# Attention sums of two units at once, with half blocks as 64-row products and TensorE in order of emission

## The chip, the cores and the metric

The kernel runs on one core of a Trainium2 chip. The metric is the device time of one execution in microseconds. A profiled execution gives the trace; its times are microseconds from the span's start.

The core has TensorE (PE; its loading of stationary operands is PEld), VectorE (DVE), ScalarE (ACT), GpSimd (POOL) and SyncE (SP), which issues the DMAs here. A matrix product on TensorE takes a stationary and a moving operand from SBUF and adds into a bank of PSUM; VectorE and ScalarE read the banks.

## The reference

Windowed causal attention, then a two-layer MLP with a gelu, over 8 batches of 576 tokens, 8 heads of 64:

```
scores = q @ k^T / 8 + alibi bias;  only the 128 keys up to and with the query count
attn   = softmax(scores)            (+ 1e-9 in the denominator)
x      = (attn @ v), heads side by side -> [4608, 512]
out    = gelu(x @ w_in) @ w_out     (w_in 512 x 2048, w_out 2048 x 512)
```

All is float32 outside. Inside, most operands are split into a high and a low float16 part (hi, lo), and a product is three float16 products: hi*hi, hi*lo, lo*hi.

## The kernel before

**Two tilings.** The MLP works on 9 tiles of 512 tokens (`t`), attention on 8 batches of 576 (`b`). A batch's 9 blocks of 64 queries (`j`) fall on two tiles: part 0 on tile `b`, part 1 on tile `b + 1` (`blocks_of`). A query block sees three key blocks of 64, its own and the two before. Heads are worked in pairs; a unit is one head pair of one batch, so a batch has four units, 0 to 3.

**A unit's way.** `scores` (L496) writes 9 groups of 128 x 192 scores into five PSUM banks; its matmuls use 64 rows and 64 columns of the array, with four of them going round (two heads, two halves of the output). `biased` (L548) scales the scores on VectorE and adds the bias; that frees the banks. `softmax` (L633) takes maxima on VectorE, exponentials on ScalarE, the high weights on GpSimd; `low_weights` (L652) makes the low parts on VectorE, and a DMA transposes the weights from `e_main` into `et` (L658), keys on partitions: 128 keys to a slot. `weigh` (L675) sums the values: the stationary operand is 128 keys x 64 features of one head (`vbuf`), the moving one the turned weights of one block of 64 queries, or of two neighbouring blocks (128 columns) where both are in the part, and a unit's results lie in two banks, one per part. Of the 128 keys of a slot a block often sees the upper or the lower 64 alone; the other half holds zeros. `leave` (L708) copies a bank to `x` as hi on ScalarE (L720) and lo on VectorE (L721, recorded at the helper's line L218).

**Order.** The first two tiles and batches follow an order written out by hand. From tile 2 on a loop (L1250) goes through 32 steps a tile, `t` = 2 to 6 with batch `b = t + 1`. Steps 0 to 15 are `mlp_in` (12 products of 512 columns into `h`, L747) and `gelu`; steps 16 to 31 are 12 products each of `mlp_out` (`o`, L793). In between, units' scores come after the products of steps 2, 11, 16 and 21 (`SCORES_AT`; tile 2: the first at 4, batch 7: the last at 22) and their sums and leaving after steps 12, 20, 30 and 30 (`WEIGH_AT`; tile 2: the first at 13). This is an order of emission: a scheduler puts each engine's instructions in order by a simulated time line, emission order being the priority. An engine works through its own list strictly in that order. Tile 7 has no attention, and tile 8 is worked by other functions.

**Banks.** PSUM's eight banks are two pools of four. `att` holds the first, second and fourth of a unit's score banks, and the sums; `mm` holds the other two score banks (`FIFTH`), `h` and `o`.

## Time and profile before

| | us |
|---|---|
| three runs: median (lowest to highest) | 880.13 (879.61 to 880.25) |
| the profiled execution, its span | 879.11, 877.3 |
| TensorE busy in the span | 861.7 (98%) |
| VectorE busy | 709.3 (81%) |
| ScalarE busy | 546.5 (62%) |
| GpSimd busy | 196.0 (22%) |
| products h (L747), busy | 337.7 |
| products o (L793), busy | 258.3 (192.4 + 65.9) |
| attention sums av (L700), busy | 42.7 |

Busy time of a group is the union of its instructions' times, so matmuls that run beside each other are not counted twice. A line of the timeline is a run of like instructions of one engine: its start, how long until the last one's end, the line, the operation, the names, the first one's shape, and the count. A matmul's end lies some 0.2 to 0.4 us behind its start, so what a run costs is read from its start to the next run's start.

### The profile page before, as it was taken

To read this page: it belongs to the slowest core of one execution; us is meant where nothing else is said; L and a number is where in the kernel's file an instruction comes from. 1 tells how busy PE (TensorE), PEld (TensorE's weight loads), DVE (VectorE), ACT (ScalarE), POOL (GpSimd) and SP (SyncE) were. 2 spreads that over 40 slices of the span, in tenths; PEclk is the share of its full clock that TensorE was granted. 3 is DMA by queue.
4 is the path that set the end of the run, shared out by engine and by line. 5 is a ranking of instruction groups with operands and counts; after the bars stand their busy time and mean duration, and the time that the engine had idled before them with its cause. 6 is when DMAs were issued, how large, how long until landed. Compare 5 with 4: busy or idle time off the path is not lost.

```text
span 877.3 us, 18582 instructions
## 1 busy us (share of the span) xinstructions
PE 861.7 (98%) x7428; PEld 476.9 (54%) x7428; DVE 709.3 (81%) x1388; ACT 546.5 (62%) x1147; POOL 196.0 (22%) x412
## 2 busy tenths in 40 slices
PE   6999999999999999999999999999999999999998
PEld 4644445544554545454545545445545554588887
DVE  6999999999768984887578775878477889998871
ACT  8999879896755573465464455466355338644760
POOL 0011000222015440452126421543054310000000
PEclk9999999999999999999999999999999999999999
DMA  9766645452572346233622473225122330001001
GB/s 311 268 208 230 228 117 133 134 168 62 132 233 38 73 97 203 57 69 77 187 72 56 93 171 117 55 55 118 39 56 56 78 67 13 0 13 37 1 1 49
DMA packets 174598, 91.63 MB, mean 104 GB/s; under 512 B 133680, under 2 KB 156336, under 8 KB 174384
## 3 DMA queue, kind: packets, MB, share of 16 engines
q1 hardware_dynamic: 174512, 90.45, 38.3%
q8 instruction: 58, 0.95, 0.4%
q14 instruction: 28, 0.23, 0.1%
HBM read 46.53 MB, written 9.44 MB: 64 GB/s over the span
## 4 chain that ended last, share of the span: by engine, by line
PE 70%; DVE 12%; ACT 2%; DMA 2%; issue 2%; POOL 1%; SPq 0%; ACTq 0%; POOLq 0%; DVEq 0%
PE h L747 27%; PE o L793 24%; PE av L700 4%; PE u_out L1082 4%; PE sc L529 3%; PE u L995 2%; DVE e_main L218 2%; DMA et<-e_main 2%; PE v L995 2%; DVE nmax L638 1%; DVE s L555 1%; PE z_out L1082 1%; PE x_out L1082 1%; PE y_out L1082 1%; PE v_out L1082 1%
## 5 line engine op out<-in xcount | busy, mean ns | idle before, releaser
L747 PE MATMUL h<-x,wi 128*128 128x512 f16 x1536 | 337.7, 379 | 1.1 <-ACT g L769 0.6
L747 PEld LDWEIGHTS <-wi 128*128 128x128 f16 x1536 | 148.5, 98 | 181.2 <-issue 4.0
L793 PE MATMUL o<-wo,g 128*128 128x512 f16 x864 | 192.4, 379 | 0.0
L793 PEld LDWEIGHTS <-g 128*128 128x128 f16 x1152 | 110.9, 98 | 132.8 <-issue 0.3
L641 ACT ACTIVATE s<-s,nmax 128x192 f32<-128x192 f32 x252 | 110.8, 441 | 46.3 <-DVE nmax L638 46.1
L218 DVE SCALAR_TENSOR_TENSOR e_main<-s,z,e_main 128x192 f16<-128x192 f32 x252 | 116.3, 505 | 15.2 <-POOL e_main L650 10.4
L771 POOL TENSOR_SCALAR g<-g,sg 128x512 f16<-128x512 f32 x96 | 76.8, 806 | 228.0 <-ACT g L769 200.8
L769 ACT ACTIVATE g<-h,gs 128x512 f32<-128x512 f32 x96 | 64.0, 686 | 95.9 <-PE h L747 59.1
L218 DVE SCALAR_TENSOR_TENSOR g<-g,sg,g 128x512 f16<-128x512 f32 x96 | 80.1, 851 | 34.0 <-POOL g L771 33.8
L650 POOL TENSOR_SCALAR e_main<-s,z 128x192 f16<-128x192 f32 x180 | 89.1, 514 | 66.9 <-ACT s L641 37.9
L555 DVE SCALAR_TENSOR_TENSOR s<-sc,cs,bias_h 128x384 f32<-128x384 f32 x112 | 64.2, 608 | 10.1 <-PE sc L529 9.9
L793 PE MATMUL o<-wo_first,g 128*128 128x512 f16 x288 | 65.9, 379 | 0.0
L720 ACT ACTIVATE x<-av,cx 128x448 f16<-128x448 f32 (+6 forms) x52 | 24.3, 481 | 62.0 <-PE av L700 59.5
L790 PE MATMUL o<-zo,g 128*128 128x512 f32 x128 | 57.0, 597 | 0.0
L638 DVE TENSOR_REDUCE nmax<-s 128x5 f32<-128x960 f32 (+1 forms) x56 | 56.6, 1043 | 0.4 <-POOL s L561 0.3
L529 PE MATMUL sc<-kbuf,qbuf 64*64 64x192 f16 (+3 forms) x1656 | 48.3, 250 | 7.6 <-ACT qbuf L431 4.4
L561 POOL MEMSET s<- 64x128 f32 (+1 forms) x112 | 19.2, 172 | 142.3 <-DVE s L555 131.2
L218 DVE SCALAR_TENSOR_TENSOR x<-av,cx,x 128x448 f16<-128x448 f32 (+6 forms) x52 | 24.7, 493 | 28.5 <-ACT x L720 28.4
L641 ACT ACTIVATION_READ_ACCUMULATOR s<-s,nmax 128x1 f32 x252 | 47.1, 187 | 0.0
L700 PEld LDWEIGHTS <-vbuf 128*64 128x64 f16 x1680 | 40.4, 111 | 9.4 <-issue 8.8
L700 PE MATMUL av<-et,vbuf 128*64 128x128 f16 (+1 forms) x1680 | 42.7, 210 | 0.4 <-DMA et<-e_main 0.3
L1082 PEld LDWEIGHTS <-g 128*128 128x128 f16 x384 | 37.6, 98 | 4.6
(269 smaller groups left out, 1126.3 us busy)
## 6 DMA issues: line engine op xcount, KB each, us to landing
v<-vp SPq DMA_DIRECT2D x32, 320.0 KB, 5.2
out<-ob SPq DMA_DIRECT2D x34, 256.0 KB, 2.2
raw<-w_in SPq DMA_DIRECT2D x8, 1024.0 KB, 11.0
raw<-w_out SPq DMA_DIRECT2D x8, 1024.0 KB, 6.7
q<-qp SPq DMA_DIRECT2D x7, 1152.0 KB, 6.0
k<-kp SPq DMA_DIRECT2D x7, 1152.0 KB, 7.5
qbuf<-qp SPq DMA_DIRECT2D x4, 288.0 KB, 5.4
kbuf<-kp SPq DMA_DIRECT2D x4, 288.0 KB, 5.7
```

The costliest lines, as they stand in the source:

```text
L218: return nc.vector.scalar_tensor_tensor(out=dst, in0=src, scalar=scale, in1=high, op0=ALU.mult, op1=ALU.subtract)
L529: done = nc.tensor.matmul(ps[bank][o, n, gap:W], a, m[:, gap:W], start=(i == 0 and (n == 0 or b > 0)), stop=(i == len(terms) - 1 and b > 0 ...
L555: yield nc.vector.scalar_tensor_tensor(out=s[:, bank[0] : bank[0] + k, :], in0=ps[bank][:, 0:k, 0:W], scalar=cs, in1=bias.broadcast_to([P, ...
L638: yield nc.vector.tensor_reduce(out=nmax[:, r], in_=s[:, r], axis=AX.X, op=ALU.max, negate=True)
L641: yield nc.scalar.activation(s[:, i, :], s[:, i, :], AF.Exp, bias=nmax[:, i : i + 1], accum_out=z[:, i : i + 1])
L650: yield nc.gpsimd.tensor_scalar(e[:, i, 0, c], s[:, i], z[:, i : i + 1], 1.0, op0=ALU.mult, op1=ALU.mult)
L700: done = nc.tensor.matmul(av[r, (j - blocks[0]) * QB : (j - blocks[0] + len(js)) * QB], v32s[b][:, hp, kb, r] if b < EXACT else vbuf[:, vi ...
L747: done = nc.tensor.matmul(ph, wi[n][:, a, cc, k * P : (k + 1) * P], x[:, cc, b, :], start=(i == 0), stop=(i == 3 * NCC - 1),)
L769: yield nc.scalar.activation(g32, ph, AF.Gelu, scale=gsc[t, n])
L771: yield nc.gpsimd.tensor_scalar(g[:, r, 0], g32, gsg[t, n], 1.0, op0=ALU.mult, op1=ALU.mult)
L793: done = nc.tensor.matmul(o, g[:, r, a, c], wo[n][:, b, k, :], start=(fc == first and i == 0), stop=(fc == last and i == 2),)
L1082: nc.tensor.matmul(ps[name][:, tb], f(d, a)[:, k, tb * P : (tb + 1) * P], w(d, b, k), start=first, stop=True, skip_group_check=True,)
```

## The change

A new function sums the values for two units at a time, from batch 3 on (in batch 7 for units 0 and 1 alone; units 2 and 3 keep `weigh` and `leave`). Every product has 64 columns, one block of queries. Where a block sees only 64 of the 128 keys of a slot, the product takes 64 rows: even blocks the lower 64, odd blocks from 3 on the upper 64. Results lie in up to four banks of `att`: by part, and within it by even and odd blocks, each with both units side by side. The list of products: for the two units and the three terms, the lower halves of both heads, after each pair of them (as long as there are any) a pair of upper halves; then the full ones. The generator stops once, between halves and full ones.

```
+    def weigh_two(one, two):
...
+        for part, odd in banks:
+            one.av[part, odd] = bank_of([P, TT], "att" if b else "mm", f"av{one.u}_{b + part}_{odd}")
...
+        low = [(st, u, t, j // 2, 1, j) for st, u, t in each for j in range(0, NB, 2)]
+        high = [(st, u, t, (j - 3) // 2, 0, j) for st, u, t in each for j in range(3, NB, 2)]
+        for n, (st, u, t, *at) in enumerate(low):
+            for h in range(2):
+                job(slice(0, D), st, u, h, *t, *at)
+            if n < len(high):
+                st, u, t, *at = high[n]
+                for h in range(2):
+                    job(slice(D, P), st, u, h, *t, *at)
+        halves = len(todo)
+        for st, u, t in each:
+            for j in range(1, NB):
+                for h in range(2):
+                    job(slice(0, P), st, u, h, *t, (j - 1) // 2, j % 2, j)
+        started = set()
+        for n, (key, o, a, m) in enumerate(todo):
+            if n == halves:
+                yield done
+            left[key] -= 1
+            done = nc.tensor.matmul(o, a, m, start=key not in started, stop=left[key] == 0, skip_group_check=True)
+            started.add(key)
+        yield done
```

Leaving takes one copy per bank for both units on ScalarE, and one low part per bank and unit on VectorE:

```
+    def leave_two(one, two):
...
+                yield nc.scalar.activation(dst(0, (0, 1)), av, AF.Copy, scale=c)
+                for u in range(2):
+                    yield low_part(dst(1, (u,)), av[:, u], c, dst(0, (u,)))
```

In the loop, units 0 and 1 are summed after step 18 (tile 2: 19) and units 2 and 3 after step 30; in batch 5 the half blocks come one step before that. The loop runs under an order of emission for TensorE:

```
-    SCORES_AT, WEIGH_AT = (2, 11, 16, 21), (12, 20, 30, 30)
+    SCORES_AT, WEIGH_AT, APART = (2, 11, 16, 21), (18, 30), (5,)
...
+        with tc.manual_schedule(engines={mybir.EngineType.PE}):
+            for step in range(2 * NFC):
...
-            for hp in range(NPAIR):
-                if weigh_at[hp] == step:
-                    for part in range(2):
-                        run(weigh(unit(b, hp), [part]))
-                        run(leave(unit(b, hp), [part]))
...
+                for n, at in enumerate(weigh_at):
+                    two = [unit(b, 2 * n + k) for k in range(2)]
+                    if n and b == B - 1:
...
+                        continue
+                    if step == at - (b in APART):
+                        weighing = weigh_two(*two)
+                        next(weighing)
+                    if step == at:
+                        next(weighing)
+                        run(leave_two(*two))
```

## Rows read from the trace of the kernel before

**Rows 1.** The page: busy time, share, instructions; the granted clock in 40 slices.
```profile
PE 861.7 (98%) x7428; PEld 476.9 (54%) x7428; DVE 709.3 (81%) x1388; ACT 546.5 (62%) x1147; POOL 196.0 (22%) x412
...
PEclk9999999999999999999999999999999999999999
```
**Rows 2.** The page: the chain that ended last, by engine.
```profile
PE 70%; DVE 12%; ACT 2%; DMA 2%; issue 2%; POOL 1%; SPq 0%; ACTq 0%; POOLq 0%; DVEq 0%
```
**Rows 3.** Two stretches of tile 4, 460 to 519 us: busy us by engine, summed.
```profile
sum 59.00, PE 59.00 PEld 29.24 DVE 50.31 ACT 32.86 POOL 28.35; mean PE 29.50 PEld 14.62 DVE 25.16 ACT 16.43 POOL 14.18
```
**Rows 4.** Timeline of TensorE in batch 4: start us, us, engine, line, operation.
```profile
392.94 1.28 PE L529 MATMUL sc<-kbuf,qbuf 64*64 64x192 f16 x54
394.14 7.94 PE L793 MATMUL o<-wo,g 128*128 128x512 f16 x36
401.93 2.75 PE L793 MATMUL o<-wo_first,g 128*128 128x512 f16 x12
404.61 1.55 PE L700 MATMUL av<-et,vbuf 128*64 128x128 f16 x54
406.09 2.76 PE L793 MATMUL o<-wo,g 128*128 128x512 f16 x12
...
433.41 2.91 PE L700 MATMUL av<-et,vbuf 128*64 128x128 f16 x108
436.25 0.39 PE L793 MATMUL o<-wo,g 128*128 128x512 f16 x1
```
**Rows 5.** Timeline of TensorE in batch 5.
```profile
475.25 1.60 PE L700 MATMUL av<-et,vbuf 128*64 128x128 f16 x66
...
498.91 1.60 PE L700 MATMUL av<-et,vbuf 128*64 128x128 f16 x66
500.44 2.76 PE L793 MATMUL o<-wo,g 128*128 128x512 f16 x12
...
527.75 3.00 PE L700 MATMUL av<-et,vbuf 128*64 128x128 f16 x132
530.69 0.39 PE L793 MATMUL o<-wo,g 128*128 128x512 f16 x1
```
**Rows 6.** Groups by shape: low parts of leaving, count, busy us, mean ns.
```profile
L218 DVE SCALAR_TENSOR_TENSOR x<-av,cx,x 128x320 f16<-128x320 f32 x8 | 4.4, 545 | 7.9 <-ACT x L720 7.9
L218 DVE SCALAR_TENSOR_TENSOR x<-av,cx,x 128x256 f16<-128x256 f32 x8 | 3.8, 477 | 6.5 <-ACT x L720 6.4
...
L218 DVE SCALAR_TENSOR_TENSOR x<-av,cx,x 128x192 f16<-128x192 f32 x8 | 3.2, 411 | 6.2 <-ACT x L720 6.2
...
L218 DVE SCALAR_TENSOR_TENSOR x<-av,cx,x 128x128 f16<-128x128 f32 x4 | 1.4, 342 | 6.0 <-ACT x L720 6.0
```
**Rows 7.** Transposing DMAs (L658), 460 to 490 us: first and last issue, landing.
```profile
L658 SPq DMA_TRANSPOSE et<-e_main x4: 1589/2094/2562, 463.5 to 487.7; - x4
...
DMA to landing us min/median/max: 3.7/3.9/4.5
```
**Rows 8.** Timeline of VectorE in batches 5 (two rows), 3 and 4.
```profile
488.70 0.60 DVE L218 SCALAR_TENSOR_TENSOR x<-av,cx,x 128x384 f16<-128x384 f32 x1
...
491.65 1.13 DVE L555 SCALAR_TENSOR_TENSOR s<-sc,cs,bias_h 128x384 f32<-128x384 f32 x2
...
314.41 0.93 DVE L218 SCALAR_TENSOR_TENSOR x<-av,cx,x 128x320 f16<-128x320 f32 x2
...
409.51 1.14 DVE L555 SCALAR_TENSOR_TENSOR s<-sc,cs,bias_h 128x384 f32<-128x384 f32 x2 [1.74 <-PE sc L529]
```
**Rows 9.** Timeline of TensorE in batch 3, with a wait.
```profile
283.65 5.34 PE L747 MATMUL h<-x,wi 128*128 128x512 f16 x24 [0.57 <-ACT g L769]
...
314.22 1.49 PE L529 MATMUL sc<-kbuf,qbuf 64*64 64x192 f16 x54
315.65 0.61 PE L793 MATMUL o<-wo,g 128*128 128x512 f16 x2
```

## The prediction

> **What bounds the kernel now.** The first view is the page's busy shares with the clock line: TensorE is busy 98% of the span, VectorE 81%, and the granted clock is full from end to end [rows 1]. The second is the chain that ended last: 70% of it is TensorE [rows 2]. The third is the stretch view, for the change touches one stage, tiles 2 to 6, and the shares of the whole span need not hold there: in 59 us of tile 4, TensorE works all 59.0 us, VectorE 50.3, ScalarE 32.9 [rows 3]. So a microsecond less on TensorE shortens the run, unless TensorE then has to wait for somebody; VectorE, the next, has 15% to spare. The fourth is TensorE's order of time: products stand without a gap, and the attention sums (av, L700) and scores (sc, L529) are bursts between them [rows 4, 5].

> The profiled execution took 879.11 us (span 877.3, 1.8 around it), 1.02 below the median of 880.13. Sums are made against 879.11 and carried over to the median by adding 1.02.

> **What a burst costs now.** From its first start to the next product's start a burst of sums takes 1.48 us with 54 matmuls (batches 4 and 6) and 1.53 with 66 (3 and 5); the two units at the end of a batch take 2.84 with 108 and 2.94 with 132 [rows 4, 5]. Ahead of it 0.09 are lost: 12 o products before a burst take 2.68 us, where 36 without one after them take 7.79, or 2.60 for 12 [rows 4]. The second half of a double burst adds 2.84 - 1.48 = 1.36 (even batches) or 2.94 - 1.53 = 1.41 (odd). By the code a unit of an even batch is 21 head pairs of 128 columns and 6 of 64, one of an odd batch 15 and 18; the two equations give 56 ns a wide pair and 32 ns a narrow one. What is left is 0.21 us per burst for getting into it and out (1.48 - 1.36 + 0.09).

> What changes costs now, with the 0.09: an even batch 2 x 1.57 + 2.93 = 6.07, an odd one 2 x 1.62 + 3.03 = 6.27, the first two units of batch 7 (60 matmuls each, between the two kinds) 1.60 each. Together 2 x 6.07 + 2 x 6.27 + 3.2 = 27.9 us.

> **What it costs then.** Two units become 192 matmuls of 64 columns: by the order of the list 18 quartets (both heads on the lower 64 rows, both on the upper), 12 pairs on the lower rows alone, 48 pairs on all 128. Sixty pairs at 32 ns are 1.92 us. A quartet of 64 columns occurs nowhere before. The score matmuls are quartets of mostly 192: 392.94 to 394.14 with the 0.09 ahead, less 0.21, is 1.08 us for 13.5 quartets, 80 ns each, and 192 columns at the rate of the o products (7.79 us for 36 of 512) are 81 ns [rows 4]. So there four tiles ran at once. The bounds for 64 columns are 27 ns (that column rate) and 64 (two pairs one after the other); I take 33, because the quartets of 192 paid nothing for being four: 0.59 us. The step from 64-row to 128-row products inside a burst is new: 0 to 0.21, I take half, 0.1. Two units: 1.92 + 0.59 + 0.21 + 0.1 = 2.82. In batch 5 the halves are a burst of their own, one step earlier: 2.51 + 2 x 0.21 = 2.93. Seven double bursts at 2.82 and two at 2.93 are 25.6 us: 2.3 saved, part by one burst less per batch, part by the upper half blocks running beside the lower.

> [...]

> **The other edits.** TensorE in order of emission costs nothing by itself: the trace already has scores, o x36, o x12, av, o x12 [rows 4], which is what the loop emits from step 16 on; what it takes away is that a late burst can be passed. Leaving two units: ScalarE keeps 4 copies, with as many columns. VectorE goes from 4 low parts to 8, of 342 ns at 128 columns, 411 at 192, 477 at 256, 545 at 320 [rows 6]. For batch 3 that is 2 x (411 + 3 x 342) = 2.9 us where 2 x (545 + 477) = 2.0 were: +0.8 for two units, 1.7 a batch, into the 15% that VectorE has free. It costs nothing while no bank and no x is waited for. At a batch's end the cover is 12 o products (2.6 us) and the six h products (1.3) that come before x's third feature block is read; a chain of a copy and four low parts, the copy taken like a low part, needs some 2.2. If that cover goes, the first h waits.

> **The new waits.** The sums now take four score banks at once, at step 18 (19 in batch 3, 17 in batch 5), and need the turned weights of unit 1. Behind a late one all products are queued, as TensorE keeps its order.
> Batch 5: the burst at 498.91 ended step 20; three steps of 2.6 and 0.09 before it, at 491.0, step 17 ended. Without the first unit's burst at 475.25 [rows 5] that is 1.62 earlier, 489.4. Unit 1's last transposing DMA went out at 487.7 and took 3.7 at the least, to 491.4 [rows 7]; VectorE read the last score bank of unit 2 that the sums need until 492.2, the first of its two reads at 491.65 [rows 8]. Both chains lose a low part of unit 0 ahead of them (0.60 [rows 8]), and gelu inputs come up to 1.62 earlier, so the wait is between 0 and 1.9; I take 0.6, nearer to the end that has both reliefs. Batches 4, 6 and 7 have a step more, 2.6 us: no wait.
> Batch 3: unit 3's scores waited already, 1.43 us to the next product [rows 9] against 1.20 [rows 4], for unit 1's leaving, which VectorE did at 314.4, behind the e_main low parts [rows 8]. The sums come a step earlier now but put twice the low parts into that queue: 0 to 1.5. I take the 0.2 as gone and nothing new.
> Total: -2.3 - 0.2 + 0.6 = -1.9: 877.2 for the profiled execution, 878.2 for the median.

> **Rivals.**
> 1. *The banks come late.* For it: 1.7 us a batch are added on VectorE, and forced order lets nothing pass. Against: in batch 4 VectorE stood idle for 1.74 us just before unit 3's scores [rows 8], room for most of the new low parts. With 1.9 in batch 5, 1.3 in batch 3 and 0.7 in the others together, 3.9 - 2.3 = +1.6 at worst; half of these waits gives -0.3, 879.8.
> 2. *Quartets of 64 columns run as two pairs* (the slower side). Place: 18 quartets in each of nine double bursts; price 31 ns each, 5.0 us: 883.2. It turns the sign from 33 + 1.9/0.162 = 45 ns a quartet on. Against it stand the score quartets; for it, that each tile changes its weights three times as often as there.
> 3. *No wait at all, and cheap changes of mode.* Quartets at 27 (-1.0), inner step 0 (-0.7), no wait in batch 5 (-0.6), and batch 3's 0.57 for ScalarE [rows 9] gone too: 875.3 at the end, with half of it 876.8.
> [...]

> **Numbers.** Chances: forecast 0.48 (877.0 to 879.2), late banks 0.25, quartets as pairs 0.12, no wait 0.13, floor 0.02. A difference under 0.2% (1.76 us, so 878.4 to 881.9) counts as no change, about what a measurement of this kernel can tell. Faster: three quarters of the forecast and all of rival 3, 0.49. Slower: rivals 2 and 4 and a quarter of the late banks, 0.20. Same: the rest, 0.31. The range goes from near rival 3's far end to rival 2: 875.6 to 883.2.

> **What would show it.** Double bursts of 192 matmuls, some 2.7 us from the first start to the next product's, two per batch (four short ones in batch 5); 3.3 means quartets as pairs. TensorE's waits: av in batch 5 under 1 us, for VectorE's reading or the transposing DMA; sc in batch 3 none. VectorE's busy time up by some 7 us. The forecast is wrong if TensorE's waits in tiles 2 to 6 pass 2 us, or if a tile's first h waits for x.

## Result and the profile after

The changed kernel takes 885.44 us (median of 6 runs, 884.83 to 886.59) against 880.19 of the kernel before on the same chip: ratio 1.0061, 95% interval 1.0048 to 1.0074. It is slower by 5.3 us, where 2 us less were forecast, and it lies above the forecast's range (875.6 to 883.2). The profiled execution took 884.83 us with a span of 883.0, that is 5.7 over the span of before.

The page of the kernel after, the lines that answer to [rows 1] and [rows 2]: busy time by engine, the granted clock, the chain that ended last.
```profile
PE 860.3 (97%) x8076; PEld 474.9 (54%) x8076; DVE 714.5 (81%) x1422; ACT 543.4 (62%) x1146; POOL 197.4 (22%) x412
...
PEclk9999999999999999999999999999999999999999
...
PE 53%; DVE 23%; ACT 6%; issue 4%; DMA 2%; POOL 1%; SPq 0%; POOLq 0%; ACTq 0%; DVEq 0%
```
TensorE is busy 1.4 us less, as a cheaper sum should make it, and the clock is as full as before. But the chain now runs through VectorE for 23% of the span where it was 12%. TensorE waits, and the stretch view says how much. The columns are the stretch, its length, and the busy time (and count) of TensorE, its weight loads, VectorE, ScalarE and GpSimd; first the kernel before, then the one after.
```profile
300.00:700.00 400.00, 399.99 (x3560) 199.30 (x3559) 300.37 (x626) 209.23 (x469) 139.07 (x288) 1.00 0.38 92
```
```profile
300.00:700.00 400.00, 393.01 (x4205) 195.02 (x4206) 299.18 (x649) 204.46 (x467) 139.14 (x285) 1.00 0.37 91
```
In these 400 us TensorE of before stands still for 0.01 us, that of after for 7.0. TensorE's waits in the kernel after (line, what ended the wait, sum, times, longest) name the places:
```profile
PE h L825 <- DVE x L218: 5.5, 4, 1.6
...
PE av L757 <- issue: 0.9, 1, 0.9
...
PE sc L529 <- DVE x L218: 0.4, 1, 0.4
```
None of the three is in the list of before (the scores' wait of before, 1.43 us from start to start against 1.20, does not show in it). The first is the forecast's own sign of failure: "if a tile's first h waits for x". It comes once at the head of each of batches 4 to 7. The timeline of TensorE at the end of batch 3 in the kernel after (start, us, engine, line, operation):
```profile
339.05 2.78 PE L757 MATMUL av<-et,vbuf 64*64 64x64 f16 x192
341.76 2.76 PE L871 MATMUL o<-wo,g 128*128 128x512 f16 x12
344.36 1.89 PE L825 MATMUL h<-x,wi 128*128 128x512 f16 x8
347.86 2.32 PE L825 MATMUL h<-x,wi 128*128 128x512 f16 x10 [1.61 <-DVE x L218]
```
The sums are done at 341.7. Then come 12 o products and 8 h products as cover (the forecast had counted 6; two more read only the high part of the third feature block of x), and the ninth h product stands for 1.6 us, because the low part of that block is not written. ScalarE, then VectorE, in the same 8 us show why:
```profile
341.62 2.43 ACT L421 ACTIVATE vbuf<-v,scv 128x2560 f16<-128x2560 f32 x1 [12.90 <-PE av L757]
343.95 1.66 ACT L782 ACTIVATE x<-av,cx 128x256 f16<-128x256 f32 x4
...
344.08 2.88 DVE L218 SCALAR_TENSOR_TENSOR vbuf<-v,scv,vbuf 128x2560 f16<-128x2560 f32 x1 [10.18 <-ACT vbuf L421]
346.88 2.29 DVE L218 SCALAR_TENSOR_TENSOR x<-av,cx,x 128x128 f16<-128x128 f32 x8
```
Both engines take the split of the next batch's v (L421 and the first L218, 2.43 and 2.88 us) ahead of the leaving (L782 and the x8). It can go first because the last 16 sums of a burst, those of the term (1, 0), read the low half of vbuf alone: the high half is free some 0.1 us before the leaving could begin (the split starts 2.57 us after the burst, 341.62 less 339.05; the leaving, where it stands first, 2.66 us after it, in the first experiment), and the four copies of the leaving stand behind it in ScalarE's list. Until then both engines were idle for 12.90 and 10.18 us.

In the kernel before the same split stands in the same place, at the end of batch 4 (ScalarE, then VectorE):
```profile
434.14 0.47 ACT L720 ACTIVATE x<-av,cx 128x256 f16<-128x256 f32 x1 [11.06 <-PE av L700]
435.00 0.98 ACT L720 ACTIVATE x<-av,cx 128x320 f16<-128x320 f32 x2 [0.38 <-PE av L700]
436.08 2.43 ACT L421 ACTIVATE vbuf<-v,scv 128x2560 f16<-128x2560 f32 x1
438.41 0.51 ACT L720 ACTIVATE x<-av,cx 128x320 f16<-128x320 f32 x1
...
435.56 0.94 DVE L218 SCALAR_TENSOR_TENSOR x<-av,cx,x 128x320 f16<-128x320 f32 x2 [0.43 <-ACT x L720]
438.54 2.88 DVE L218 SCALAR_TENSOR_TENSOR vbuf<-v,scv,vbuf 128x2560 f16<-128x2560 f32 x1 [2.03 <-ACT vbuf L421]
441.34 0.55 DVE L218 SCALAR_TENSOR_TENSOR x<-av,cx,x 128x320 f16<-128x320 f32 x1
```
There three of four leavings are ahead of it, as unit by unit and part by part their banks finished earlier; the one behind it is the last unit's second part, for a tile that is read a batch later. With the sums of two units mixed, all banks finish within the last matmuls, and all leavings fall behind the split.

What each burst costs over plain products is worked out for all bursts alike: the time from the start of the product before it to the start of the product after it, less one product's pace (216 ns); the last three rows are differences to before.

| term | forecast, us | measured, us |
|---|---|---|
| one whole double burst | 2.82 | 2.805 (all seven) |
| batch 5's two in parts | 2.93 each | 3.18 and 3.98, of it 0.28 for banks and 1.06 without a releaser |
| all these sums, waits in them included | -2.3 + 0.6 | -1.1 (27.93 to 26.79) |
| scores of batch 3's unit 3 | -0.2 | +0.6 (1.52 to 2.15) |
| first h of batches 4 to 7 | 0 | +6.2 (gaps of 1.34, 1.78, 1.92, 1.99, less 4 x 0.22) |
| all | -1.9 | +5.7 |

The gaps go from start to start; the view of the waits gives 5.5 for the same four, as it counts from the modelled end of a product.

The second new wait, TensorE at the end of batch 5 in the kernel after (answers to [rows 5]):
```profile
527.84 1.14 PE L757 MATMUL av<-et,vbuf 64*64 64x64 f16 x96
528.92 2.76 PE L871 MATMUL o<-wo,g 128*128 128x512 f16 x12
531.61 1.32 PE L757 MATMUL av<-et,vbuf 128*64 128x64 f16 x71
533.80 0.60 PE L757 MATMUL av<-et,vbuf 128*64 128x64 f16 x25 [0.87 <-issue]
```
After 71 of 96 matmuls TensorE stands for 1.06 us, start to start, and waits for no semaphore ("issue"). The third, TensorE and VectorE at batch 3's unit 3 (answers to [rows 8, 9]):
```profile
313.78 0.27 PE L529 MATMUL sc<-kbuf,qbuf 64*64 64x192 f16 x1
314.43 1.27 PE L529 MATMUL sc<-kbuf,qbuf 64*64 64x192 f16 x53 [0.38 <-DVE x L218]
...
312.14 1.06 DVE L218 SCALAR_TENSOR_TENSOR e_main<-s,z,e_main 128x192 f16<-128x192 f32 x3
313.13 2.28 DVE L218 SCALAR_TENSOR_TENSOR x<-av,cx,x 128x128 f16<-128x128 f32 x8
```
The scores need a bank that the leaving still reads, and VectorE takes the leaving at 313.13, behind low parts of e_main: the wait that was there before is longer, not gone.

### The profile page after: what moved, and what is told of

Same layout as the page of the kernel before. It is cut to its first block, busy times and chain, and to the rows that moved or that the text cites. A ratio compares the mean times of both kernels' runs of the same rounds, so it can differ in the third digit from the quotient of the medians.

```text
span 883.0 us, 19916 instructions
## 1 busy us (share of the span) xinstructions
PE 860.3 (97%) x8076; PEld 474.9 (54%) x8076; DVE 714.5 (81%) x1422; ACT 543.4 (62%) x1146; POOL 197.4 (22%) x412
## 3 DMA queue, kind: packets, MB, share of 16 engines
q8 instruction: 63, 1.03, 0.5%
## 4 chain that ended last, share of the span: by engine, by line
PE 53%; DVE 23%; ACT 6%; issue 4%; DMA 2%; POOL 1%; SPq 0%; POOLq 0%; ACTq 0%; DVEq 0%
PE h L825 20%; PE o L871 16%; DVE e_main L218 6%; PE u_out L1160 4%; DVE g L218 3%; DVE s L555 3%; ACT s L641 2%; PE u L1073 2%; PE sc L529 2%; PE av L757 2%; DVE nmax L638 2%; DMA et<-e_main 2%; PE v L1073 2%; PE z_out L1160 1%; PE v_out L1160 1%
## 5 line engine op out<-in xcount | busy, mean ns | idle before, releaser
L218 DVE SCALAR_TENSOR_TENSOR e_main<-s,z,e_main 128x192 f16<-128x192 f32 x252 | 116.7, 508 | 15.7 <-POOL e_main L650 10.8
L218 DVE SCALAR_TENSOR_TENSOR g<-g,sg,g 128x512 f16<-128x512 f32 x96 | 81.1, 863 | 31.9 <-POOL g L849 31.8
L529 PE MATMUL sc<-kbuf,qbuf 64*64 64x192 f16 (+3 forms) x1656 | 48.2, 250 | 7.8 <-ACT qbuf L431 4.4
L218 DVE SCALAR_TENSOR_TENSOR vbuf<-v,scv,vbuf 128x2560 f16<-128x2560 f32 x7 | 20.2, 2887 | 36.9 <-ACT vbuf L421 36.9
L421 ACT ACTIVATE vbuf<-v,scv 128x2560 f16<-128x2560 f32 x7 | 17.0, 2432 | 41.0 <-PE av L757 41.0
L868 PEld LDWEIGHTS o<-zo,g 128*128 128x128 f32 x128 | 23.8, 190 | 27.5 <-issue 25.8
L529 PEld LDWEIGHTS <-qbuf 64*64 64x64 f16 x1512 | 30.2, 107 | 15.7 <-issue 12.9
```

Of the source, the lines that this page charges most:

```text
L218: return nc.vector.scalar_tensor_tensor(out=dst, in0=src, scalar=scale, in1=high, op0=ALU.mult, op1=ALU.subtract)
L529: done = nc.tensor.matmul(ps[bank][o, n, gap:W], a, m[:, gap:W], start=(i == 0 and (n == 0 or b > 0)), stop=(i == len(terms) - 1 and b > 0 ...
L868: done = nc.tensor.matmul(o, g[:, r, c], zo[n][:, n % 2, k * DM : (k + 1) * DM], start=(fc == first), stop=(fc == last))
```

## The experiments

Ratios are to the kernel before, run on the same chip beside each. All are one edit on the changed kernel but for three: both edits at once, and the two mixed kernels at the end.

**The terms of a sum in another order** (e1_terms).
```diff
-        terms = ((None, 0),) if b < EXACT else ((0, 0), (0, 1), (1, 0))
+        terms = ((None, 0),) if b < EXACT else ((1, 0), (0, 0), (0, 1))
```

> The changed kernel with the three terms of the sums in another order: (lo v, hi w) first, the two terms on v's high half last. Theory A: in the changed kernel the last term reads only the low half of vbuf, so the high half is free some 0.5 us before the banks are done, and the scheduler puts the next batch's 2.4 us copy of v (L421) and its 2.9 us low part ahead of the leaving; the first h of four tiles waits for that, 6.2 us over its normal pace. With v's high half in use to the end the leaving stands first: the waits of h for x go from 5.5 us to none, 885.4 - 6.2 = 879.2 (878.6 to 880.0). Theory B: the leaving of two units (4 copies, 8 low parts) is itself too long for the 3.9 us of cover: h still waits half or more, 882 or above.

879.34 us (878.37 to 880.67), ratio 0.9994 (0.9985 to 1.0003): 6.1 us under the changed kernel (5.8 when each is set against the kernel before of its own runs), even with the one before. TensorE, ScalarE and VectorE at the end of batch 3 in this kernel:
```profile
339.54 2.78 PE L757 MATMUL av<-et,vbuf 64*64 64x64 f16 x192
...
344.85 7.50 PE L825 MATMUL h<-x,wi 128*128 128x512 f16 x34
...
342.20 1.68 ACT L782 ACTIVATE x<-av,cx 128x256 f16<-128x256 f32 x4 [12.99 <-PE av L757]
343.75 2.44 ACT L421 ACTIVATE vbuf<-v,scv 128x2560 f16<-128x2560 f32 x1
...
342.71 2.29 DVE L218 SCALAR_TENSOR_TENSOR x<-av,cx,x 128x128 f16<-128x128 f32 x8 [8.32 <-ACT x L782]
346.23 2.88 DVE L218 SCALAR_TENSOR_TENSOR vbuf<-v,scv,vbuf 128x2560 f16<-128x2560 f32 x1 [1.22 <-ACT vbuf L421]
```
With the high half of vbuf read to the end, the split can't be early; the leaving goes first, and TensorE has no gap there (the h products run in one stretch from 344.85) nor at the three heads after it. One of 0.5 us is left at the head of tile 7, behind batch 7, where the changed kernel had 0.1. The order of three terms was worth some 6 us.

**The parts one after the other** (e8_parts_in_turn), the terms as they were.
```diff
-        for st, u, t in each:
-            for j in range(1, NB):
-                for h in range(2):
-                    job(slice(0, P), st, u, h, *t, (j - 1) // 2, j % 2, j)
+        for part in range(2):
+            for st, u, t in each:
+                for j in range(1, NB):
+                    if where[j][0] == part:
+                        for h in range(2):
+                            job(slice(0, P), st, u, h, *t, (j - 1) // 2, j % 2, j)
```

> One edit on the changed kernel, the terms left as they are: the full 128-row products of a sum of two units go part by part (all of the batch's first tile, then all of its second), so the first tile's two banks are done some 0.6 us before the burst ends, ahead of the last term's end. Theory A (the split of the next batch's v goes ahead of the leaving on ScalarE and VectorE because the high half of v is free before the banks are): the leaving of the first tile's banks goes ahead of the split, only that of the second tile's stands behind it, and that tile is read a whole batch later. The waits of the first h for x at the heads of batches 4 to 7 (5.5 us in the sum of waits) go, at least 4.5 of them: 879.5 to 880.8 beside a kernel before of about 880. Rival B (the leaving itself, two units at once, is too long for the cover, whatever stands before it): the chain of 1.66 us of ScalarE and four low parts of 1.25 is as long as before, so at least 1 us of each of the four waits stays: 883 or more.

879.9 us (878.45 to 881.05), ratio 0.9998 (0.9989 to 1.0006). A second lever at the same spot gives the same 5.5 us. ScalarE at the end of batch 3 in this kernel:
```profile
341.26 0.94 ACT L784 ACTIVATE x<-av,cx 128x256 f16<-128x256 f32 x2 [12.36 <-PE av L759]
342.09 2.43 ACT L421 ACTIVATE vbuf<-v,scv 128x2560 f16<-128x2560 f32 x1
344.41 0.84 ACT L784 ACTIVATE x<-av,cx 128x256 f16<-128x256 f32 x2
```
Half of the leaving is ahead of the split, half behind it, as in the kernel before. All four waits are gone, though the leaving has as many instructions: rival B falls. (The stop in batch 5 is 1.55 us in this kernel's profile, 0.5 more than in the changed one.)

**TensorE's order left to the planner** (e3_order_free).
```diff
-        with tc.manual_schedule(engines={mybir.EngineType.PE}):
+        with nullcontext():
```

> One edit on the changed kernel: TensorE's order is no longer that of emission, the planner sets it. The order differs in four places only, where the first few score products stand ahead of a block of h. Theory A: the waits at the heads of the batches come from ScalarE's and VectorE's order, which is the same here, so they stay: the same time within 1.0 us (884.5 to 886.5). Rival C (the forced order itself holds TensorE up, as the prediction's document has it as one of the parts): 2 us or more come back, 883 or less.

882.74 us (880.89 to 884.19), ratio 1.0036 (1.0022 to 1.005). Theory A as it was put (no more than 1 us) fell, and rival C's number came. The profiled execution was the quickest of its five runs; TensorE and VectorE at the end of batch 3 in it:
```profile
340.93 2.76 PE L871 MATMUL o<-wo,g 128*128 128x512 f16 x12
343.53 5.34 PE L825 MATMUL h<-x,wi 128*128 128x512 f16 x24
348.80 0.54 PE L529 MATMUL sc<-kbuf,qbuf 64*64 64x192 f16 x10
...
343.24 2.88 DVE L218 SCALAR_TENSOR_TENSOR vbuf<-v,scv,vbuf 128x2560 f16<-128x2560 f32 x1 [10.18 <-ACT vbuf L421]
346.05 2.29 DVE L218 SCALAR_TENSOR_TENSOR x<-av,cx,x 128x128 f16<-128x128 f32 x8
```
The leaving is as late as in the changed kernel, and still no h waits there. In the program's list the planner has laced three blocks of h together: 6 products of each of the three first, which read only the two feature blocks of x that are there, then 6 that read the high part of x's third feature block, then 10 score products, then the rest. So the late leaving costs 6.2 us only together with the order of emission, which forbids the lacing. The freedom has its own price: four groups of scores are cut in two (1.7 us in their sum of costs), and batch 5's first sums wait 1.2 us more for their banks.

**Both at once** (e12_terms_and_order_free), the edits of the first and the third experiment.

> Both edits at once: the terms with vlow first (879.3 alone) and the planner's order in place of the order of emission (882.7 alone; there the planner interleaved three blocks of h at the heads of batches 4 to 7, so that no product waited for x, but cut four groups of scores in two). With the terms turned the planner's order differs from that of emission only in 1 to 6 products of h exchanged at the same heads. Theory A2 (the order of emission costs only because a late leaving stands ahead of it; with the leaving early there is nothing to pass): the same as the turned terms alone, 879.3 within 0.8 (878.5 to 880.1). Rival C (the forced order costs something of its own, 2.7 us as in the run where it alone was undone): 876.6 to 877.5. Rival F (the planner's order costs by itself, as the cut scores did): 881 or more.

878.96 us (877.95 to 880.7), ratio 0.9992 (0.9983 to 1.0002). Of the four combinations of terms and order, the change, with the late leaving and the forced order, lies at 885.4, the other three at 879.3, 882.7 and 879.0. Once the leaving is early the forced order costs nothing measurable: theory A2.

**Batch 5's halves not apart** (e2_not_apart).
```diff
-    SCORES_AT, WEIGH_AT, APART = (2, 11, 16, 21), (18, 30), (5,)
+    SCORES_AT, WEIGH_AT, APART = (2, 11, 16, 21), (18, 30), ()
```

> The changed kernel with batch 5 not apart (APART empty). Its four bursts cost 7.16 us over the products in the profile, whole bursts elsewhere 2.81 each: 885.4 - 1.55 = 883.9 if the 1.0 us stop inside its last burst (no semaphore awaited, an instruction fetch just before it) and the 0.3 at its first are of the split alone. If the supply of instructions stops a whole burst in the same place, some 1 us comes back: 884.9 or more. Theory A and B alike leave the waits of h as they are.

886.44 us (885.14 to 887.45), ratio 1.0072 (1.006 to 1.0085). The forecast of a gain fell, and the other branch came (884.9 or more, if a whole burst is stopped in the same place). TensorE at the two bursts of batch 5 in this kernel:
```profile
495.31 2.49 PE L757 MATMUL av<-et,vbuf 64*64 64x64 f16 x173
499.07 0.50 PE L757 MATMUL av<-et,vbuf 128*64 128x64 f16 x19 [1.26 <-issue]
...
532.00 2.40 PE L757 MATMUL av<-et,vbuf 64*64 64x64 f16 x167
535.98 0.60 PE L757 MATMUL av<-et,vbuf 128*64 128x64 f16 x25 [1.58 <-issue]
```
Each now stops once, for 1.46 and 1.78 us start to start, with no releaser; the other seven whole bursts don't. The part of the change that puts the halves apart mends two thirds of a stop that nobody had named (3.2 us in two, against 1.06).

**Halves as 128-row products** (e4_full_rows).
```diff
-                job(slice(0, D), st, u, h, *t, *at)
+                job(slice(0, P), st, u, h, *t, *at)
...
-                    job(slice(D, P), st, u, h, *t, *at)
+                    job(slice(0, P), st, u, h, *t, *at)
```
The products take the other half's rows in too, which hold zeros, as the kernel before does; number and order of the instructions stay, and so do the sums.

> The changed kernel with the half blocks as 128-row products (the other 64 rows multiply zeros), so that no two row halves run beside each other. If the quartets of 64 columns run at once as the burst of 2.80 us says (some 32 ns each), each becomes two pairs of 32: 162 x 31 ns = +5.0, less up to 0.7 for the change of mode inside the burst: 889.7 to 890.4, and a whole burst of 3.2 to 3.3 us. Rival (quartets run as pairs already): no change, 885.4.

888.7 us (888.32 to 890.15), ratio 1.0102 (1.0088 to 1.0115), 1.0 below the expected range, though a burst costs what was expected; 0.4 of it is a shorter wait of unit 3's scores in batch 3. TensorE at batch 3's second sums:
```profile
340.43 3.23 PE L757 MATMUL av<-et,vbuf 128*64 128x64 f16 x192
```
A whole burst costs 3.254 us against 2.805. The 96 matmuls of the halves are 18 quartets and 12 pairs; as 48 pairs they cost 0.45 more, though this kernel is spared the step from 64-row to 128-row products (0.09 in the kernel after, see below). So, as an estimate, a quartet saves (0.45 + 0.09) / 18 = 30 ns against two pairs of 32, which leaves 34, where 33 was taken and rival 2 had 64. At that price the quartets do run four at once; rival 2 falls.

**The old sums at the new places** (e6_old_sums): two units one after the other with L700 and the old leaving, at the new steps and in forced order.
```diff
-                    if step == at - (b in APART):
-                        weighing = weigh_two(*two)
-                        next(weighing)
                     if step == at:
-                        next(weighing)
-                        run(leave_two(*two))
+                        for st in two:
+                            for part in range(2):
+                                run(weigh(st, [part]))
+                                run(leave(st, [part]))
```

> The changed kernel with the old sums and leaving of single units at the new places (both units after step 18 and after step 30), in TensorE's forced order. Bursts by the profile of before: 2.94 or 3.03 for two units, nine of them 26.9 against 27.9: -1.0. By theory A only the last leaving, for the tile after next, comes behind the split of v, as in the kernel before, so no h waits: 879.2 (878.7 to 880.2). If places and forced order by themselves cost something, 881 or more.

879.48 us (877.97 to 880.65), ratio 0.9994 (0.9985 to 1.0003). No h waits for x at the heads of batches 4 to 7, and no sum stops: a double burst costs 2.94 to 3.03, all of them 26.86. So of the 27.93 of before 1.07 go with the places alone (one burst less per batch); the new form of the sums is worth another 0.13 to 0.22 a burst.

**The borders moved** (e10_moved_borders). The page of the kernel after has 63 packets of instructions (queue q8) with 1.03 MB, 16 KB each, and 16,152 matmuls and weight loads on TensorE (8,076 of each); that of before has 58 packets and 14,856 (7,428 of each). These are 256 for each packet in both, and 259 for each of the 5 more, so the packets are taken as pieces of TensorE's program, 256 instructions of 64 bytes in each, as an estimate. Counted in TensorE's list, all three stops above, one in the changed kernel and two in e2, come at the same place in a piece of 256, and so does the one below, within two. This kernel has the terms of e1, batch 3's first sums a step earlier, and batch 5 so:
```diff
-    SCORES_AT, WEIGH_AT, APART = (2, 11, 16, 21), (18, 30), (5,)
+    SCORES_AT, WEIGH_AT, APART = (2, 11, 16, 21), (18, 30), ()
...
+        if b == 5:
+            weigh_at[0] += 4
...
-                    if n and b == B - 1:
+                    if n and b in (5, B - 1):
```

> On the kernel with the terms in the order that was tried first (vlow first: 879.3): batch 3's first sums one step earlier, so that their leaving is done before unit 3's scores; batch 5's first sums whole at step 22 in place of apart at 17 and 18; batch 5's second sums unit by unit as in the kernel before. Supply theory (TensorE stops where a program of 64-byte instructions crosses a border of 256 instructions, if it came to that border faster than the 16 KB behind it were fetched; the stops so far were at the second border within one burst, 256 instructions after a first that lay 79 to 115 instructions into it): batch 5's first burst now starts so that only one border falls into it, 143 instructions in, and has no stop (2.81 us net, where e1 had 1.45 and 1.73); the second, 240 instructions, has none (2.9 to 3.0). But the following bursts are moved by 120 instructions: that of batch 7 now has borders 115 and 371 instructions in and gets a stop of 0.7 to 1.8 us in its last 10 matmuls, those of batch 6 (35 and 291, 23 and 279) may have one too. Sum: -0.6 (batch 3) -1.1 (batch 5) +0.7 to +5: 878.4 to 882.7. Rival D (the stops belong to batch 5, its data or its transfers): none in batches 6 and 7, 877.7.

883.82 us (883.0 to 884.92), ratio 1.0042 (1.0029 to 1.0055), above the expected range. TensorE in batch 5's second sums, and in batch 7's new burst:
```profile
531.39 1.89 PE L700 MATMUL av<-et,vbuf 128*64 128x128 f16 x66 [3.10 <-DMA et<-e_main]
...
684.14 2.65 PE L757 MATMUL av<-et,vbuf 64*64 64x64 f16 x184
687.97 0.32 PE L757 MATMUL av<-et,vbuf 128*64 128x64 f16 x8 [1.17 <-issue]
```
Batch 5 has lost its stops, and batch 7, which never had one, has got one of 1.37 us in the last ten matmuls, where the moved border lies: the stops belong to the place in the program, not to batch 5. The two bursts of batch 6, with borders 35 and 291, and 23 and 279 instructions in, have none. The rest of the overrun is a wait of its own: with batch 5's first sums four steps later, unit 3's turned weights come 3.1 us late, which was not foreseen. And after TensorE had stood for that time its granted clock was 0.50 for 3.4 us, in which an o product takes 0.43 us in place of 0.22; by the length of the stretch that cost another 1.7 us, an estimate. The stretch view of this kernel has it (the third number from the end):
```profile
532.50:535.90 3.40, 3.40 (x30) 1.68 (x25) 1.11 (x2) 2.90 (x2) 0.00 (x0) 0.50 0.00 0
```

**The better version** (e11_best): the terms of e1, batch 3's first sums one step earlier, both of batch 5's sums in the old form at steps 18 and 30.
```diff
-            scores_at[0], weigh_at[0] = scores_at[0] + 2, weigh_at[0] + 1
+            scores_at[0], weigh_at[0] = scores_at[0] + 2, weigh_at[0]
...
-                    if n and b == B - 1:
+                    if b == 5 or n and b == B - 1:
```

> The same with both of batch 5's sums unit by unit as in the kernel before, at steps 18 and 30, so the bursts of batches 6 and 7 have one border each, 143 to 235 instructions in. Supply theory: no stop anywhere; batch 5 costs 2 x 2.95 = 5.9 in place of e1's 6.86 (-0.95), batch 3's scores -0.6: 877.8 (877.0 to 878.6), against about 880 of the kernel before and 885.4 of the changed one. Rival D (the stops belong to batch 5): the same here, 877.8. Rival E (the old form keeps batch 5's banks until scores or sums wait for them): 0.5 to 2 us of waits in batch 5, 878.4 to 880.

878.03 us (876.77 to 879.28) against 879.8, ratio 0.9978 (0.9969 to 0.9987): faster than both kernels. The stretch view of this kernel, and TensorE at batch 3's sums and unit 3's scores, and at batch 5's two sums:
```profile
300.00:700.00 400.00, 399.79 (x4155) 199.59 (x4155) 306.49 (x653) 208.06 (x471) 141.81 (x291) 1.00 0.38 93
```
```profile
305.19 0.29 PE L757 MATMUL av<-et,vbuf 64*64 64x64 f16 x12
305.69 2.68 PE L757 MATMUL av<-et,vbuf 64*64 64x64 f16 x180 [0.21 <-DVE s L555]
...
316.17 1.39 PE L529 MATMUL sc<-kbuf,qbuf 64*64 64x192 f16 x54
...
493.23 3.00 PE L700 MATMUL av<-et,vbuf 128*64 128x128 f16 x132
...
528.66 3.00 PE L700 MATMUL av<-et,vbuf 128*64 128x128 f16 x132
```
TensorE stands for 0.2 us of the 400. Batch 3's scores no longer wait for the leaving (net 1.42), at the price of 0.4 us in which its sums wait for banks; batch 5's sums run without a stop. By the net costs the sums are 26.08 (27.93 before) and the scores 26.80 (26.90): -1.95, and -1.8 was measured. (The profiled execution itself, with a span of 877.5, was no shorter than that of before, 877.3: it was 2.0 us behind when the first scores of the loop began, 264.37 against 262.37, and made up 2.0 from there to the end of batch 7's sums.)

## Why the prediction was wrong

**The failed step** is the leaving at the batch's end: "the cover is 12 o products (2.6 us) and the six h products (1.3) ... a chain of a copy and four low parts ... needs some 2.2", costed at nothing. The cover is there in the timeline after, and the leaving alone fits into it: with nothing ahead of it (e1) its first copy starts at 342.20 and its last low part ends at 345.00, before the ninth h product is due. What was left out is what else those two engines would do in that time: 2.43 and 2.88 us of the split of v, which came ready in the same tenth of a microsecond. It stood in the trace of before, and the prediction did not read ScalarE's timeline at that place; it asked whether the chain fits the cover, not what would stand in front of it. With the split ahead the ninth h product can start 6.1 us after the burst (341.76 to 347.86), against 4.3 of cover (12 and 8 products, to 346.09). Over four heads that is +6.2 us, shown by two levers (e1, e8) that put the leaving back in front.

**The order of emission** was costed at nothing "by itself", with the remark that it takes away that a late burst can be passed. It was not a late burst but a late leaving, and what could have been passed are the last products of an h block. Alone undone it brings back 2.7 us of the median, on top of an early leaving nothing (e3, e12): the two factors make the loss only together.

**The sums** were forecast at 2.82 a burst and cost 2.805; the quartets ran four at once, at 34 ns by e4. The inner step, from 64-row to 128-row products, is the start gap between the last of the halves and the first full product, 0.122 us at batch 3's second sums where gaps of 0.023 to 0.028 stand around it: 0.09 more, where 0.1 was taken, and not the 0.21 of entering and leaving a burst. For the floor that has 0.02 among the chances no run shows a smallest distance of starts; the 192 starts of that burst lie 14 ns apart on average (2.71 us from 339.05 to 341.76). The size of the saving was wrong by a term that the prediction didn't have: TensorE stops in batch 5 for 1.06 us with no wait shown.

**Batch 5's banks** cost 0.28 where 0.6 was taken. (The upper bound of 1.9 there does not follow from its rows, by which it is 2.2: 492.2, less the low part's 0.60, less 489.4. It decided nothing.) **Batch 3's scores**, taken as rid of 0.2, wait 0.6 longer: of the bounds 0 to 1.5 the lower was chosen, although the row put the leaving behind the e_main low parts and the change puts twice as many into that queue; e11 shows that a step earlier ends it. **VectorE** grew by 5.2 us, about 7 were forecast.

The sum: 6.2 (leaving) + 1.1 (stop) + 0.8 (batch 3) - 0.3 (batch 5's banks) - 0.2 (sums) = 7.6, from -1.9 to +5.7. None of the rivals was the cause: late banks came nearest, with the right engine, but in other places.

Why some borders of the program stop a burst and others don't can be read from the times of the instruction packets in the traces (packets and borders paired from the last one back). In the kernel after, the packet before the stop went out at 531.52, 3.3 us after TensorE had passed the border before; from 528.3 to 531.5 other transfers kept the DMA engines 87% busy. It landed at 532.40, and TensorE went on at 533.80, 1.40 later. There are nine stops in these runs: in all six kernels with batch 5 apart the same matmul is held, for 0.7 to 1.6 us, two are in e2 and one in e10. All nine end 1.2 to 1.6 us after the landing of the packet that went out at the border before; the other borders from tile 2 on, some 500 in the eleven kernels, were reached 1.5 us or more after that landing. The author's reading of these times is that a burst stops where it comes to a border too soon after that packet. In batch 5's parts the packet went out late, 2.9 to 3.6 us after its border (elsewhere at most 1.9). In the whole bursts that stop it went out 1.0 to 1.5 us after a border well inside the burst, and the burst was through the next 256 instructions in some 2 us; where the first border lies at a whole burst's start, the packet had gone out 1.3 to 3.1 us ahead of it.

What stays open: no run changes the fetch alone. That it is what TensorE waits for is argued from places and times that fit; no row shows the wait itself.

## What to carry to other kernels

A cover is not free time: before a wait is costed at nothing, read what each engine of the chain already has queued or coming ready in that stretch, and which of the two the planner may put first; a large off-path operation freed a moment too early (here a 5 us split of the next batch's input) can cost more than the change saves: 6.2 us, where 1.9 were forecast to be saved. Let the last reader of a shared buffer be the last instruction of a burst if its successor is not urgent. Merging work so that all results end together takes away the stagger that hid their follow-up, and a fixed order of instructions takes away the means to cover it.
